# Two-layer attention decode: whole key blocks, one softmax for both head groups, queries made block-diagonal in PSUM, and an instruction order given as a table

## The chip, the cores and the metric

The kernel runs on 1 core of one Trainium2 chip. The metric is the device time of one run in microseconds (us), and of several runs the median.

## The reference

Two rounds of the same two layers with the same weights: attention of one new token per batch over a sliding window of cached keys and values, then a feed-forward layer, each with a layer norm ahead and a residual around it. All data are bfloat16.

```python
# B=8, Sq=1, D=448, Hq=16, Hkv=8, Sk=4096, Dh=256, F=1792
W = min(4096, max(256, Sk // 4))                      # 1024
q = (x @ wq).reshape(B, Sq, Hq, Dh)                   # two query heads per key head
k = jnp.repeat(k_cache[:, :, Sk - W:, :], 2, axis=1)  # v alike
p = softmax(einsum("bhqd,bhkd->bhqk", q, k) * Dh ** -0.5)
attn = einsum("bhqk,bhkd->bhqd", p, v).reshape(B, Sq, Hq * Dh) @ wo
ffn = silu(x @ w1) @ w2
x = x + attn(layernorm(x)); x = x + ffn(layernorm(x))
x = x + attn(layernorm(x)); x = x + ffn(layernorm(x))
```

The products, norms and residuals are small. The weights are some 10 MB, and the keys and values in the window 67 MB (8 batches of 8 heads of 1024 x 256, for keys and for values).

## The kernel before, in words

**Data.** Each batch's keys and values are 16 slots of 512 KB (one key head each). Both rounds use them, so they are loaded once, into a ring of 30 slots in SBUF ([128 x 2048] bfloat16 each). SyncE issues every DMA in one order: x, wq, the keys and values of batch 0, wo, w1, w2, and then K0..K7, V0..V7 of batches 1 to 7. A load waits until the slot that it takes is free: `layer2` (L1266) marks key slots as free after round 2's scores and value slots after round 2's products with values, and `pump` (L1229) then issues the next loads. Not more than 10 half slots are outstanding (`dma`, L656). `load_k` (L708) and `load_v` (L716) bring a slot as two halves of 256 KB with 2 KB rows. `load_wq` (L671) brings three full chunks of 1 MB and two pieces of 64 partitions, each 256 KB.

**One batch.** The batches are worked one after the other, with neighbours overlapped. Round 1 (`layer1`, L1240): VectorE turns each half key slot in place in 32 x 32 blocks of 32-bit words (L1246, 16 turns a batch). `scores` (L881) multiplies block-diagonal queries (`qbd`) with them: in round 1 both groups of four key heads in one product of 512 columns, in round 2 (layer 2 in the code) one group at a time, 256 columns. The softmax (L895 to L937) takes the row maximum on VectorE (L892), spreads it with two 32 x 32 turns (L900, L905), computes one exponential per head group on ScalarE (L912), turns the weights by products with the identity (`pT`, L918), copies them (`pTev`, L927) and sums them by eight small products (L931); a reciprocal follows (L936). The products with values are L951. Their result goes through a ScalarE copy (L956), another turn by products (L958) and VectorE copies (L965, L971) into `oT`; seven value heads take that way, the eighth goes by columns (L985, L991). Products with wo (L1002 by rows, L1008 by columns) add up in banks 6 and 7, `fold` (L1018, L1019) brings the rows into columns beside the residual (`x_init`, L997).

**Feed-forward and queries.** `xb_evac` copies the residual column in two steps (L1029 for 384 rows, L1030 for the last 64, which have a mask) and a third (L1057) for the second half of w1. `stat` (L1036, L1040) makes sums for the norm; `rsqrt` (L749 to L765) does the inverse root, on VectorE for the feed-forward's norm and on GpSimd for round 2's. w1 is L842, its turn L851, then L1063 to L1074 (tanh form of silu), and w2 is L1002 again. `chain` then copies the residual for the query product (L1086 to L1088), multiplies with wq in two head groups (L1104), turns the result (L1109), selects each head's part with four fp32 products (L1115), adds the mean's part on VectorE (L1121) and masks it into block-diagonal queries (L1129; VectorE for the first group, GpSimd for the second). Both groups of L1104 write bank 6, so the second waits for the first's turn. The exponential carries the norm's inverse deviation as its scale, and L909 scales the maximum.

**End.** Round 2's attention leaves `oT2` for all eight batches. `final` multiplies it with wo (L1135), starts the residual with a product (L1153), folds (L1165), copies (L1168 to L1172) and does the last feed-forward for all eight batches at once; the output leaves from L1219 and L1220.

**Order.** Each engine runs its own list in order; semaphores hold an instruction until what it needs is there. The lists come from a planner at build time (`Plan.schedule`, `tails`, `best_schedule`) that simulates the kernel with costs, shifted by hand-set numbers (`OFFSETS`, `MOVES`, `HOLDS`). Where the planner sees TensorE idle it places a filler (L1290): a product whose result nobody reads.

```python
        if last:
            softmax(b, 1, (k2,), sc, k2 == 1)
```

These two lines of `layer2` mean that the last batch runs round 2's softmax one head group at a time; all others run it once for both.

## Time and profile before

| | before |
|---|---|
| median of 3 runs | 241.93 us (241.26 to 241.96) |
| span of the profiled execution | 239.7 us |
| TensorE products (PE) | 194.1 us, 81%, 3567 of them, 129 fillers among them |
| TensorE weight loads (PEld) | 97.3 us, 41% |
| VectorE (DVE) | 152.8 us, 64%, 425 instructions |
| ScalarE (ACT) | 86.5 us, 36%, 292 |
| GpSimd (POOL) | 26.0 us, 11%, 125 |
| moved by DMA | 78.22 MB, mean 326 GB/s |
| mean granted TensorE clock | 0.986 of full speed |

The span goes from the first to the last instruction of one profiled execution; the run's time holds a little more. Busy time is what the instructions of an engine take; TensorE overlaps its products, and its weight loads run beside them. In the rows below, a line number names the kernel's line, `out<-in` its tiles, `x15` a count; after the bar stand the total busy time and the mean of one in ns, and after a second bar the time that the engine was idle ahead of them, with what released it. In tables by stretches, a row is a window in us, then its length and for PE, PEld, DVE, ACT and POOL the busy time (and instructions), the granted clock, the share of the 16 DMA engines and GB/s.

### The profile page before, as it was taken

How to read it: one execution, taken by the hardware profiler on the slowest of the kernel's cores; microseconds unless marked ns; L12 is line 12 of the kernel's file. 1: busy time of each engine (PE TensorE's matmuls, PEld its weight loads, DVE VectorE, ACT ScalarE, POOL GpSimd, SP SyncE). 2: the span in 40 equal slices, each digit the busy share in tenths (PEclk: the TensorE clock that was granted, in tenths of full speed). 3: DMA queues.
4: the chain of work that ended last, by engine and by line, in shares of the span. 5: the costliest groups of instructions: out<-in, count | busy, mean ns of one | idle time of the engine just before them, and what ended most of it. 6: DMA issues, size and time to landing. Idle time of an engine off the chain costs nothing.

```text
span 239.7 us, 8472 instructions
## 1 busy us (share of the span) xinstructions
PE 194.1 (81%) x3567; PEld 97.3 (41%) x3567; DVE 152.8 (64%) x425; ACT 86.5 (36%) x292; POOL 26.0 (11%) x125
## 2 busy tenths in 40 slices
PE   1052358878989899989898898989898999899894
PEld 1051123232345344535433453454344535445552
DVE  7339620037955995996599669946985996334533
ACT  2001231033045516532734354355416440544331
POOL 6100000002010031004001200310031003003000
PEclk9999985999999999999999999999999999999999
DMA  6999999999999999999999999999999999200000
GB/s 228 373 355 403 404 402 384 378 374 406 402 405 403 403 402 404 398 350 379 360 400 402 371 373 379 376 368 377 358 399 399 397 330 399 102 3 3 4 3 1
DMA packets 40341, 78.22 MB, mean 326 GB/s; under 512 B 4320, under 2 KB 6512, under 8 KB 39792
## 3 DMA queue, kind: packets, MB, share of 16 engines
q1 hardware_dynamic: 40304, 77.69, 87.2%
q8 instruction: 28, 0.46, 0.7%
q14 instruction: 9, 0.07, 0.1%
HBM read 77.67 MB, written 0.01 MB: 324 GB/s over the span
## 4 chain that ended last, share of the span: by engine, by line
PE 47%; DMA 19%; DVE 16%; ACT 7%; SPq 7%; issue 4%; POOL 0%; DVEq 0%; ACTq 0%
DMA ring<-in_A_k_cache_dram 10%; PE bank L951 9%; PE bank L881 7%; DMA w2o<-in_B_w_dram 6%; DVE ring L1246 6%; PE bank L1002 6%; PE bank L1290 5%; PE bank L1104 5%; PE bank L1115 3%; DMA ring<-in_A_v_cache_dram 3%; SPq L682 3%; ACT qT L912 2%; DVE mrow L892 2%; PE bank L918 2%; PE bank L958 1%
## 5 line engine op out<-in xcount | busy, mean ns | idle before, releaser
L1246 DVE STREAM_TRANSPOSE ring<-ring 128x512 uint32<-128x512 uint32 x128 | 81.4, 684 | 10.7 <-DMA ring<-in_A_k_cache_dram 10.7
L1290 PE MATMUL bank<-wq_sb,smalls 128*128 128x512 bf16 x129 | 38.6, 386 | 0.0
L881 PE MATMUL bank<-ring,qbd 128*16 128x512 bf16 (+2 forms) x768 | 35.8, 324 | 3.4 <-DVE ring L1246 2.3
L951 PE MATMUL bank<-ring,pT_sb 128*4 128x512 bf16 (+1 forms) x512 | 36.2, 378 | 0.1
L881 PEld LDWEIGHTS bank<-ring,qbd 128*16 128x16 bf16 (+1 forms) x768 | 19.6, 91 | 17.1 <-DVE qbd L1129 3.9
L858 ACT ACTIVATE qbd<-q1s 32x128 bf16<-32x128 bf16 x32 | 10.2, 320 | 42.9 <-PE bank L881 42.3
L892 DVE TENSOR_REDUCE mrow<-bank 128x2 f32<-128x512 f32 (+1 forms) x17 | 11.0, 646 | 11.9 <-PE bank L881 11.1
L1104 PE MATMUL bank<-wq_sb,xn 128*4 128x512 bf16 (+1 forms) x272 | 17.7, 369 | 0.9 <-ACT x2s L1091 0.5
L1018 ACT ACTIVATE qT<-bank 128x448 bf16<-128x448 f32 x16 | 8.7, 543 | 22.4 <-PE bank L1002 22.4
L951 PEld LDWEIGHTS bank<-ring,pT_sb 128*4 128x4 bf16 (+1 forms) x512 | 11.5, 84 | 11.1 <-issue 1.8
L1290 PEld LDWEIGHTS bank<-wq_sb,smalls 128*128 128x128 bf16 x129 | 10.2, 98 | 12.3 <-issue 7.6
L918 PE MATMUL bank<-ident,qT 128*64 128x16 bf16 x256 | 8.5, 180 | 7.3 <-ACT qT L912 6.6
L1002 PE MATMUL bank<-w2o,oT 128*1 128x448 bf16 x224 | 13.2, 352 | 0.7 <-DMA w2o<-in_A_wo_dram 0.7
L956 ACT ACTIVATE qT<-bank 128x512 bf16<-128x512 f32 x16 | 9.6, 597 | 9.7 <-PE bank L951 6.7
L1109 DVE STREAM_TRANSPOSE qT<-bank 128x512 f32<-128x512 f32 (+1 forms) x17 | 11.3, 664 | 2.2 <-PE bank L1104 2.0
L918 PEld LDWEIGHTS bank<-ident,qT 128*64 128x64 bf16 x256 | 6.1, 111 | 12.5 <-ACT qT L912 11.5
L956 ACT ACTIVATE qbd<-bank 128x512 bf16<-128x512 f32 (+1 forms) x16 | 9.1, 570 | 5.5 <-PE bank L951 3.3
L749 POOL TENSOR_SCALAR smalls<-smalls 128x1 int32<-128x1 int32 x8 | 1.5, 190 | 86.9 <-ACT smalls L1051 76.3
L1257 POOL MEMSET qT<- 128x64 bf16 x8 | 1.2, 152 | 82.5 <-PE bank L958 68.7
L1115 PE MATMUL bank<-qT,w2o 128*32 128x64 f32 x128 | 8.4, 352 | 2.0 <-DVE qT L1109 0.8
L912 ACT ACTIVATE qT<-bank,mrow 128x256 bf16<-128x256 f32 x17 | 7.2, 470 | 7.6 <-DVE mrow L905 7.3
L1046 DVE SCALAR_TENSOR_TENSOR smalls<-bank,smalls 128x1 f32<-128x1 f32 x8 | 1.1, 143 | 13.2 <-ACT smalls L1044 9.5
(183 smaller groups left out, 254.6 us busy)
## 6 DMA issues: line engine op xcount, KB each, us to landing
ring<-in_A_k_cache_dram SPq DMA_DIRECT2D x128, 256.0 KB, 6.2
ring<-in_A_v_cache_dram SPq DMA_DIRECT2D x128, 256.0 KB, 6.1
w2o<-in_A_wo_dram SPq DMA_DIRECT2D x2, 1792.0 KB, 13.1
wq_sb<-in_A_wq_dram SPq DMA_DIRECT2D x3, 1024.0 KB, 6.8
w2o<-in_B_w_dram SPq DMA_DIRECT2D x1, 1568.0 KB, 14.5
w_sb<-in_B_w_dram SPq DMA_DIRECT2D x3, 448.0 KB, 12.2
wq_sb<-in_A_wq_dram SPq DMA_DIRECT2D x2, 256.0 KB, 10.2
w_sb<-in_B_w_dram SPq DMA_DIRECT2D x2, 112.0 KB, 11.4
```

The lines of the kernel that those rows point to most:

```text
L881: fns.append(lambda e, cb=cb, par=par, j=j, kv=kv, m=m, c0=c0, c1=c1: e.matmul(bank[sc][32 * j:32 * j + m, c0:c1], qbd[layer][:, j * 8 + c ...
L892: dve(lambda e: e.tensor_reduce(mseg[layer][:, ks[0]:ks[-1] + 1], bank[sc][:, lo:hi].rearrange("p (k n) -> p k n", k=len(ks)), AX.X, ALU.m ...
L912: act(lambda e, k2=k2: e.activation(e_sb[ei][:, k2, :, :].rearrange("p uh (jj ul) -> p uh jj ul", ul=2), bank[sc][:, k2 * 256:(k2 + 1) * 2 ...
L918: pe([lambda e, uh=uh, ql=ql, k2=k2: e.matmul(bank[lb][64 * ql:64 * ql + 64, k2 * 64:k2 * 64 + 64].rearrange("p (j q u r) -> p u j q r", j ...
L951: fns.append(lambda e, qh=qh, uh=uh, j=j, vv=vv: e.matmul(bank[ob][32 * j:32 * j + 2 * w, 0:w * DH], p_col(ei, k2, j, qh, uh, w), vv, star ...
L956: act(lambda e: e.activation(o_sb[oi][:, 0:w * DH], bank[ob][:, 0:w * DH], ACTF.Copy), bk(ob), O_K[oi], 0.2 + w * 0.2, "oevh" if ob == OB[ ...
L1002: pe([lambda e, i=i, c=c: e.matmul(bank[XB][32 * c:32 * c + 1, 0:D], rhs(i), w_sb[:, i * D:(i + 1) * D], start=(first and i - i0 < 4), sto ...
L1104: fns.append(lambda e, j=j, c=c, wb=wb, off=off, h0=h0, n=n, k2=k2: e.matmul(bank[wb][32 * j:32 * j + 4, h0:h0 + n], xn[:, part(c, k2), j, :],
L1109: dve(lambda e, wb=wb, h0=h0, n=n: e.transpose(qT[:, h0:h0 + n].rearrange("p (c a i) -> p c a i", a=2, i=32), bank[wb][:, h0:h0 + n].rearr ...
L1115: pe([lambda e, qs=qs, j=j: e.matmul(qs[32 * j:32 * j + 32].rearrange("p (k c r) -> p k r c", k=4, c=8), irep, qT[:].rearrange("p (r c i) ...
L1246: dve(lambda e, v=v: e.transpose(v, v), [("slot", s, h)], [("slot", s, h)], 0.67, "KT")
L1290: fills = {n: [lambda e, j=j, m=P // n: e.matmul(bank[OB[0]][m * j:m * j + m, 0:2 * DH], zero_b.broadcast_to([P, m]), wq_sb[:, 0:2 * DH], ...
```

## The change

- **Keys whole.** `load_k` brings a slot in one DMA of 512 KB with 4 KB rows. VectorE turns a slot in one instruction of 128 x 1024 words, 8 a batch. `load_v` stays. The second 64-partition piece of wq is issued from ScalarE's queue at the program's start.
- **One softmax area.** Both head groups' scores add into the same 256 columns of a bank (other rows are zero through padded queries), in round 1 too, where 64 products of 256 columns replace 32 of 512. One maximum, one exponential (which also sums its row), one set of eight turning products; one fp32 product with a selection matrix makes the sums that eight made.
- **Block-diagonal in PSUM.** The second head group of wq writes bank 4, the first bank 6. Eight fp32 products, four with the mean's part (which ScalarE writes into `qbd`) and four with the turned query, make the block-diagonal queries in bank 5; one ScalarE copy with the inverse deviation as its scale moves them to `qbd`. The addition and masking on VectorE and GpSimd go, and so do L909 and the exponential's scale.
- **Residual in five columns.** The last 64 rows have a column for each half of the partitions, so that one copy replaces two or three (`xb_evac`, the copy for wq, the copy in `final`); `x_init`, products by columns and folds work on five columns. In `final` the residual is added behind the wo products.
- **Norms.** GpSimd's inverse root takes five steps instead of nine.
- **Order.** The planner goes. `ORDER` gives each engine's list as task numbers, and `place` reads it; `f` words are fillers, 101 instead of 129.

```diff
-    AHEAD, WHOLE = 10, 0
+    AHEAD = 10
 def load_k(s, b, kvh):
-        for h in range(2):
-            dma(lambda e, h=h: e.dma_start(slots[s][:, 1024 * h:1024 * h + 1024], src[:, 1024 * h:1024 * h + 1024]),
-                [("slot", s, h)], W * DH, "slot%d_%d" % (s, h), rate=400e3, ahead=AHEAD)
+        dma(lambda e: e.dma_start(slots[s], src), [("slot", s, h) for h in range(2)], 2 * W * DH, "slot%d" % s,
+            rate=418e3, ahead=AHEAD)
 def load_wq():
-                [("wq", 3 + h)], D3 * HD, "wq%d" % (3 + h), rate=220e3)
+                [("wq", 3 + h)], D3 * HD, "wq%d" % (3 + h), via=("sp", "act")[h])
 def layer1(b):
-            for h in range(2):
-                v = slots[s][:, h * 1024:(h + 1) * 1024].bitcast(U32)
-                dve(lambda e, v=v: e.transpose(v, v), [("slot", s, h)], [("slot", s, h)], 0.67, "KT")
-        for ks in ((0, 1),) if PAIR0 else ((0,), (1,)):
-            scores(b, 0, ks, SC[0])
+            v = slots[s].bitcast(U32)
+            dve(lambda e, v=v: e.transpose(v, v), [("slot", s, 0), ("slot", s, 1)], [("slot", s, 0), ("slot", s, 1)],
+                1.22, "KT")
+        for k2 in range(2):
+            scores(b, 0, k2, SC[0])
 def softmax(b, layer, ks, sc):
+        act(lambda e: e.activation(
+            e_sb[ei].rearrange("p uh (jj ul) -> p uh jj ul", ul=2),
+            bank[sc][:, 0:256].rearrange("p (ul uh jj) -> p uh jj ul", ul=2, uh=4), ACTF.Exp, bias=mseg[layer][:, 0:1],
+            scale=1.0, accum_out=es), bk(sc) + [("mseg", layer)], [("e", ei), ek], 0.55, "exp%d" % layer)
+        pe([lambda e: e.matmul(bank[lb][:, C_L + 8 * k0:C_L + 8 * k1], es.broadcast_to([P, P]), sel16[:, 8 * k0:8 * k1],
+                               start=True, stop=True)], [ek] + SEL16, bk(lb), (256, 1), "l%d" % layer)
 def xb_evac():
-        act(lambda e: e.activation(xbt[:, 0:3, 0], xcols()[:, 0:3], ACTF.Copy), bk(YB), [("xbt", 0)], 0.175, "xbt")
-        act(lambda e: e.activation(xbt[:, 3, 0:1], xcols()[:, 3:4], ACTF.Copy, scale=mask4[:, 3:4]), bk(YB) + MASK4,
-            [("xbt", 1)], 0.175, "xbt")
+        act(lambda e: e.activation(xbt[:, :, 0], xcols(), ACTF.Copy), bk(YB), ["xbt"], 0.175, "xbt")
 def chain(b):
-            parts = [(XB, 0, DH), (YB, DH, DH)] if (tail or WQS) and k2 == 0 else [(XB, 0, 2 * DH)]
+            wbs = [(XB, 0, DH), (LB[0], DH, DH)] if tail and k2 == 0 else [((XB, XB if tail else LB[0])[k2], 0, 2 * DH)]
...
+            for part_ in range(2):
+                for j in range(4):
+                    rhs = qT[:].rearrange("p (r c i) -> p i c r", r=2, i=32)[:, 0:4] if part_ else \
+                        csm[:, k2].rearrange("p (j c) r -> p j c r", j=4)
+                    fns.append(lambda e, j=j, rhs=rhs, part_=part_: e.matmul(
+                        qs[32 * j:32 * j + 32].rearrange("p (k c q r) -> p q k c r", k=4, c=8, q=4)[:, j], irep, rhs,
+                        start=not part_, stop=bool(part_), tile_position=(0, 32 * j)))
+            act(lambda e, k2=k2: e.activation(qbd[1][:, k2], qs.rearrange("p (n x) -> p n x", x=8), ACTF.Copy,
+                                              scale=rstds[1]), bk(LB[1]) + [("rstd", 1)], [("qbd", 1, k2)], 0.4, "qbd")
 ORDER = ...
+        "47 54 66 73 146 76 147+6 81 159+1 173+1 164+3 169 175+1 f1@168 f1@168 f1@106@168 163 f1@168 f2@168 178 "
...
-    pl.best_schedule(fill)
+    pl.place(fill)
```

In the fences below a row is an instruction's line, operation, tiles, shape and count. The first place is on VectorE, in batch 4's feed-forward norm; `ring` are key slots of batch 5 that are turned, `smalls` hold the norm's numbers, and bank 7 holds the sums. Before:

```order
L1246 STREAM_TRANSPOSE ring<-ring 128x512 x5
L1046 SCALAR_TENSOR_TENSOR smalls<-bank7,smalls 128x1
L749 TENSOR_SCALAR smalls<-smalls 128x1
L754 SCALAR_TENSOR_TENSOR smalls<-smalls 128x1
L1246 STREAM_TRANSPOSE ring<-ring 128x512
L760 SCALAR_TENSOR_TENSOR smalls<-smalls 128x1
L851 STREAM_TRANSPOSE qT<-bank6 128x2x224
L754 SCALAR_TENSOR_TENSOR smalls<-smalls 128x1
L1063 SCALAR_TENSOR_TENSOR vt<-cs1,smalls,qT 128x14
L760 SCALAR_TENSOR_TENSOR smalls<-smalls 128x1
```

Now:

```order
L990 STREAM_TRANSPOSE ring<-ring 128x1024 x3
L802 SCALAR_TENSOR_TENSOR smalls<-bank7,smalls 128x1
L513 TENSOR_SCALAR smalls<-smalls 128x1
L518 SCALAR_TENSOR_TENSOR smalls<-smalls 128x1
L531 SCALAR_TENSOR_TENSOR smalls<-smalls 128x1
L620 STREAM_TRANSPOSE qT<-bank6 128x2x224
L518 SCALAR_TENSOR_TENSOR smalls<-smalls 128x1
L818 SCALAR_TENSOR_TENSOR ffn<-ffn,smalls,qT 128x14
L531 SCALAR_TENSOR_TENSOR smalls<-smalls 128x1
```

Half-slot turns that stood partly among the norm's steps (five ahead, one between) are now three whole turns, all ahead of it.

The second place is on TensorE, around batch 4's product of the feed-forward with w2 (`hT` or `ffn` on the right, bank 6). `qbd1` is also the buffer for the turn of attention's output (L958, now L705), and `pT_sb1` are round 2's weights of batch 3. Before:

```order
L951 MATMUL bank1<-ring,pT_sb1 4x512 x8
L931 MATMUL bank5<-pT_sb1,smalls 128x16 x8
L1290 MATMUL bank2<-wq_sb,smalls 128x512
L958 MATMUL bank5<-ident,qbd1 128x8 x4
L1002 MATMUL bank6<-w2o,hT 1x448 x14
L958 MATMUL bank5<-ident,qbd1 128x8 x4
L1290 MATMUL bank2<-wq_sb,smalls 128x512 x2
```

Now (the w2 product is the row of L753, and L645 are round 1's scores of batch 5, which write bank 0):

```order
L698 MATMUL bank1<-ring,pT_sb1 4x512 x4
L645 MATMUL bank0<-ring,qbds 16x256 x8
L705 MATMUL bank5<-ident,qbds 128x8 x4
L645 MATMUL bank0<-ring,qbds 16x256 x8
L705 MATMUL bank5<-ident,qbds 128x8 x4
L753 MATMUL bank6<-w2o,ffn 1x448 x14
L645 MATMUL bank0<-ring,qbds 16x256 x16
```

The scores of batch 5 with its first four key heads' slots now begin ahead of the w2 product; before they began after it (next fence).

The third place follows right behind on TensorE: batch 4's queries for round 2 (L1104 with wq, now L857; L1115 the selection, now L872), up to the scores. Before:

```order
L1104 MATMUL bank6<-wq_sb,xn 4x512 x16
L1036 MATMUL bank5<-xbt 128x32 x4
L1040 MATMUL bank5<-smalls 128x16
L997 MATMUL bank7<-xb0,ident 128x64
L1290 MATMUL bank2<-wq_sb,smalls 128x512
L1115 MATMUL bank5<-qT,w2o 32x4x2x8 x4
L1104 MATMUL bank6<-wq_sb,xn 4x512 x16
L881 MATMUL bank1<-ring,qbd1 8x256 x32
L881 MATMUL bank0<-ring,qbd0 16x512 x8
L1115 MATMUL bank5<-qT,w2o 32x4x2x8 x4
L881 MATMUL bank0<-ring,qbd0 16x512 x24
```

Now:

```order
L792 MATMUL bank5<-ffn 128x32 x4
L796 MATMUL bank5<-smalls 128x16
L857 MATMUL bank6<-wq_sb,xn 4x512 x16
L857 MATMUL bank4<-wq_sb,xn 4x512 x8
L645 MATMUL bank0<-ring,qbds 8x256 x24
L872 MATMUL bank5<-qbds,w2o 32x32x2 x4
L872 MATMUL bank5<-qT,w2o 32x32x2 x4
L645 MATMUL bank0<-ring,qbds 8x256 x8
L857 MATMUL bank4<-wq_sb,xn 4x512 x8
L645 MATMUL bank1<-ring,qbds 16x256 x32
L872 MATMUL bank5<-qbds,w2o 32x32x2 x4
L872 MATMUL bank5<-qT,w2o 32x32x2 x4
```

The second group of wq products stands right behind the first, in another bank, with scores of batch 5 (L645 into bank 0) ahead of the selection; each selection has four products with `qbds` (the mean's part) and four with `qT`.

More of the change, by code (lines that the diff above doesn't have):

```diff
@@ L1 @@
-import heapq
 import numpy as np
@@ L1017, in fold @@
     def fold():
[L1018 to L1021 removed]
+        act(lambda e: e.activation(rowb, bank[XB][:, 0:D], ACTF.Copy), bk(XB), ["rowA"], 0.545, "rowb")
```

616 lines of the change are left out of this document (184 added, 432 removed), and 89 rows, old and new, of tables (MOVES, OFFSETS, ORDER).

## The prediction

> **What bounds the kernel now.** I read the page, the chain that ended last, the busy time of the engines by stretches, the waits, and the timelines of one batch and of the end. The page gives the span.
>
> ```profile
> span 239.7 us, 8472 instructions
> ```
>
> The median of the three runs shown is 241.93 us, so 2.2 us lie around the profiled span. I make the sum against the span and add 2.2. The runs lie between 241.26 and 241.96, so about 0.3%, 0.7 us, can be told from no change.
>
> The chain that ended last, in order of time (start, length, what), shows the milestones.
>
> ```profile
> 54.00 0.94 PE bank L1002 x14
> 68.98 0.70 DVE mrow L892
> 202.32 0.70 DVE mrow L892
> 205.45 1.25 PE bank L951 x19
> 237.47 0.38 DVE ring L1219
> ```
>
> L1002 at 54.00 is the first product with w2: until then the kernel waits for weights. L892 is the row maximum of layer 1, for batch 1 at 68.98 and for batch 7 at 202.32. L951 at 205.45 is batch 7's first product with its values, and L1219 is the last copy. So there are three stretches: a head of 68.98 us, six equal periods, and a tail of 37.4 us. The busy times over the six periods (length, then PE, PEld, DVE, ACT, POOL, granted clock, DMA share, GB/s), first, last and sum:
>
> ```profile
> 68.98:91.63 22.65, 20.52 (x390) 10.07 (x379) 17.14 (x45) 10.10 (x35) 2.70 (x11) 1.00 1.05 403
> ...
> 180.90:202.32 21.42, 19.90 (x395) 10.26 (x383) 17.32 (x48) 10.18 (x34) 2.61 (x11) 1.00 1.02 380
> sum 133.34, PE 121.79 PEld 60.64 DVE 103.08 ACT 60.55 POOL 15.72; mean PE 20.30 PEld 10.11 DVE 17.18 ACT 10.09 POOL 2.62
> ```
>
> A period is 133.34 / 6 = 22.22 us. TensorE is busy for 20.3 us of it, but the fillers (products that nobody reads) are in that:
>
> ```profile
> L1290 PE MATMUL bank<-wq_sb,smalls x61: 375/378/392, 69.8 to 197.1; 128*128 128x512 bf16 x61
> ```
>
> Sixty-one of them, ten a period, mark where TensorE has nothing to do and waits for a softmax, a residual copy or a turned query. The transfers are not the first bound: in the last period they run at 380 GB/s, and the waits between 69 and 202 us say why (the first is SyncE's queue, from 90 us on; us in total, times, longest).
>
> ```profile
> SPq L713 <- PE bank L951: 11.5, 5, 3.1
> DVE ring L1246 <- DMA ring<-in_A_k_cache_dram: 2.7, 4, 1.1
> ```
>
> Key loads wait 11.5 us for slots that layer 2 still reads; VectorE's turns wait only 2.7 us for keys. So a period is the serial path of one batch through TensorE, VectorE and ScalarE, and the stream follows it. What the change takes off that path counts six times.
>
> **The head.** Rates by stretches (last column GB/s):
>
> ```profile
> 6.00:8.00 2.00, 0.48 (x12) 0.40 (x12) 1.25 (x9) 0.00 (x0) 1.06 (x10) 1.00 1.02 426
> 10.00:12.00 2.00, 0.00 (x0) 0.00 (x0) 0.00 (x0) 0.00 (x0) 0.00 (x0) 1.00 1.01 266
> 12.00:14.00 2.00, 0.13 (x5) 0.16 (x6) 0.00 (x0) 0.00 (x0) 0.00 (x0) 1.00 1.02 255
> 56.00:58.00 2.00, 1.65 (x23) 0.69 (x24) 1.34 (x3) 1.42 (x11) 0.31 (x2) 1.00 1.05 406
> ```
>
> At 6 to 8 us whole rows of wq (8 KB each) move at 426 GB/s; at 56 to 58 half slots (2 KB rows) at 406. Between them, at 10 to 14, stand the two 64-partition pieces of wq, at some 260. The change issues one of these (256 KB) from ScalarE's queue at the start, beside full-width rows: at 426 it takes 0.62 us instead of 1.01, a gain of 0.4. Bounds: 0, if the piece slows its neighbours as much, and 0.75, if the piece left behind also runs at 426. The Trainium skill, DMA: Bandwidth & Descriptors (section Issuing engines are not separate DMA queues), says that DMAs from several engines interleave on the same 16 engines and that a second issuer saves only sequencer time; by that rule this term is 0 and the sum below 0.4 us higher. No run so far has two issuers, so the trace cannot decide it.
>
> Whole key slots have 4 KB rows. One of 16 engines takes 2048 B x 16 / 406 = 81 ns for a 2 KB row and 308 ns for 8 KB; a straight line between gives 156 ns for 4 KB, 419 GB/s. Keys of one batch (4.19 MB) then take 10.0 us instead of 10.3: 0.32 us for batch 0 and again for batch 1 (bounds: 0 at 406, 0.5 at 426). The turns:
>
> ```profile
> L1246 DVE STREAM_TRANSPOSE ring<-ring 128x512 uint32<-128x512 uint32 x128 | 81.4, 684 | 10.7 <-DMA ring<-in_A_k_cache_dram 10.7
> ...
> 60.79 5.44 DVE L1246 STREAM_TRANSPOSE ring<-ring 128x512 uint32<-128x512 uint32 x9
> ```
>
> Nine in a row take 5.44 us, so 605 ns apart though each lasts 684. The launch that a whole turn saves is at least nothing and, by this overlap, some 0.08 us: eight pairs, 0.6 us a batch. Against it, the last slot lands whole and its turn lasts about 1.2 us instead of 0.68: 0.5 later. Layer 1's scores add 0.2 (below). These three cancel to +0.1. Head: -0.4 - 0.32 - 0.32 + 0.1 = -0.9.
>
> **A period.** Costs in layer 1's softmax:
>
> ```profile
> L892 DVE TENSOR_REDUCE mrow<-bank 128x2 f32<-128x512 f32 x15 | 10.1, 675 | 11.1 <-PE bank L881 10.3 <-POOL qbd L1129 0.8
> L892 DVE TENSOR_REDUCE mrow<-bank 128x1 f32<-128x256 f32 x2 | 0.8, 425 | 0.8 <-PE bank L881 0.8
> L912 ACT ACTIVATE qT<-bank,mrow,smalls 128x256 bf16<-128x256 f32 x15 | 7.8, 560 | 0.3
> ...
> 114.94 0.84 ACT L912 ACTIVATE qT<-bank,mrow 128x256 bf16<-128x256 f32 x2
> ```
>
> Both head groups now lie in 256 columns: the maximum falls from 675 to 425 ns (-0.25), and two exponentials (0.84 together) become one. It also sums its row, which no row here shows; I take the dearer 256-column form, 0.56 (-0.28). TensorE's rows of batches 2 and 3, from its timeline:
>
> ```profile
> 116.50 0.37 PE L931 MATMUL bank<-pT_sb,smalls 128*128 128x16 bf16 x8
> 116.80 1.89 PE L951 MATMUL bank<-ring,pT_sb 128*4 128x512 bf16 x28
> ...
> 129.66 0.38 PE L1290 MATMUL bank<-wq_sb,smalls 128*128 128x512 bf16 x1
> 130.70 0.53 PE L1115 MATMUL bank<-qT,w2o 128*32 128x64 f32 x8 [0.66 <-ACT x2s L1091]
> ...
> 132.16 1.06 PE L881 MATMUL bank<-ring,qbd 128*8 128x256 bf16 x32
> 133.15 0.39 PE L1290 MATMUL bank<-wq_sb,smalls 128*128 128x512 bf16 x1
> 133.47 0.61 PE L881 MATMUL bank<-ring,qbd 128*16 128x512 bf16 x8
> 133.91 0.52 PE L1115 MATMUL bank<-qT,w2o 128*32 128x64 f32 x8
> 134.21 2.52 PE L881 MATMUL bank<-ring,qbd 128*16 128x512 bf16 x56
> ```
>
> Starts, not ends, are to be read, since products overlap. The eight sums (L931) hold TensorE for 0.30 us; one fp32 product takes their place, by an eighth to a quarter of L1115's time about 0.1: -0.2 in each layer, -0.4. The query selection (L1115, four fp32 products in eight records) holds it for 0.30 to 0.53 us; it now has eight products, the second four adding the mean's part in PSUM, and all eight stand behind the turned query. I take +0.4 each, twice: +0.8. Layer 1's scores were 32 products of 512 columns at 55 ns (0.44 / 8), 1.76 us; they become 64 of 256 at 31 ns (0.99 / 32), 1.98: +0.22. The fifth residual column adds six small products, at 31 ns +0.19. TensorE's own work grows by 0.81.
>
> Its gaps shrink. From 129.66 to 130.70 it had a filler and a wait of 0.66, since the second weight group shared bank 6 with the first and had to wait until that was turned. The change gives it bank 4, and next batch's scores stand there too (last pair of order fences): -1.04. The residual is copied once:
>
> ```profile
> L1030 ACT ACTIVATE xbt<-bank,smalls 128x1 bf16<-128x1 f32 x16 | 4.1, 258 | 0.1
> ```
>
> On the path to layer 2's statistics and weights -0.26. With softmax, -0.25 - 0.28 - 0.26 - 1.04 = -1.83. VectorE also loses the query's addition and masking, and GpSimd its masking; ScalarE's one copy of 256 columns replaces them while TensorE works on the second group, so I price that at 0 (about 0.5 a period if that cover goes). A period: 22.22 + 0.81 - 1.83 = 21.2; six of them, -6.1.
>
> Next bound: w2 lands just ahead of 54.00, now near 53.2. Seven batches of keys (29.4 MB at 419) and values (at 406) take 70.1 + 72.3 us, so the stream cannot end before 195.6; by the forecast batch 7's values are wanted from 197.7 to 200. It fits, barely.
>
> **The tail.**
>
> ```profile
> 217.31 0.36 PE L1013 MATMUL bank<-w2o,smalls 128*128 128x448 bf16 x1
> 218.36 0.39 PE L1290 MATMUL bank<-wq_sb,smalls 128*128 128x512 bf16 x1
> 220.08 0.41 PE L1153 MATMUL bank<-x2s,ring 128*128 128x28 f32 x2
> 222.23 0.41 DVE L1129 TENSOR_TENSOR qbd<-mrow,smalls 128x256 bf16<-128x256 f32 x1
> 223.25 0.30 ACT L909 ACTIVATE mrow<-mrow,smalls 128x2 f32<-128x2 f32 x1 [2.01 <-DVE mrow L905]
> 230.91 0.26 ACT L1169 ACTIVATE ring<-bank,smalls 128x8 bf16<-128x8 f32 x1
> ```
>
> These steps stand on the last chain and go: a filler product (0.36), another (0.32 of it), the residual's start (0.35, moved behind the last wo products), a masking that stood ahead of the maximum's transposes (0.41), the scaled bias (0.30, since queries now carry the scale), and a masked copy (0.26). With the layer 1 softmax (0.73, the sum included), layer 2's two sums (0.4) and one residual copy (0.26): -3.39. Against that +0.37 for twelve small products and +0.4 for one selection. Tail: -2.6. The scaled query needs the inverse deviation earlier; GpSimd's nine steps for it become five, which I price at 0 (0.3 if late).
>
> **Sum.** -0.9 - 6.1 - 2.6 = -9.6; span 230.1, time 232.3.
>
> **The rivals.**
> *The stream takes over.* If gaps close further (VectorE is relieved of 0.6 us in turns besides), a period falls to the stream's 20.4 and the end is set by 195.6: batch 7's values 4 us earlier than forecast, 228. For it: 403 GB/s in the first period; against it, the slot waits. Chance 0.16.
> *The gaps move instead of closing.* TensorE's added 0.81 and new waits eat what is saved: a period stays at 22.2, only head and tail gain: 238.4. For it: TensorE is already busy 20.3 of 22.2. Chance 0.20, 0.03 of it with no change at all.
> *Late keys hold the path (slower).* Layer 1's scores of batch 5 now stand ahead of batch 4's w2 product, and three whole turns ahead of its statistics (order fences). Both engines take instructions in order, so a late key slot holds batch 4's path, which frees the slots later still. Price: the longest turn wait was 1.1 us; two such a period make 2.2, six periods 13.2: 245.5. It decides from 9.6 / 6 = 1.6 us a period on. Against it: 2.7 us of such waits in all six now. Chance 0.12.
> *The clock drops.*
>
> ```profile
> 24.00:26.00 2.00, 0.17 (x7) 0.20 (x8) 2.00 (x4) 1.59 (x5) 0.00 (x0) 1.00 1.05 406
> 36.00:38.00 2.00, 1.29 (x18) 0.33 (x13) 0.17 (x1) 0.60 (x1) 0.00 (x0) 0.50 1.05 389
> ```
>
> TensorE, busy 0.17 of 2 us at 24, ran at half clock at 36. The change has 101 fillers instead of 129; if one stretch of some 7 us in the tail ran at half clock, 3.5 us: 235.8. The Trainium skill, TensorE: Matmul & The Clock Gate (section HAM oscillation), says that idle gaps longer than about 3.4 us halve the clock; the six periods have none and show 1.00. Chance 0.06.
>
> **How the numbers follow.** The forecast has 0.44 (230 to 235); 0.02 is left for the rest. Faster: 0.44 + 0.16 + 0.17 + 0.06 + 0.01 = 0.84; within 0.3%: 0.04; slower: 0.12. The range goes from the stream's bound, 227.5, to the case of moved gaps with its next microsecond, 239.5, and leaves the slower case out. Should the change not do what it says, keys at 4 KB moving no faster than 406, the head loses 0.64 and the stream's bound 2.3: 232.9, inside it.
>
> **What would show it.** Maxima of layer 1 about 21.2 us apart, batch 7's near 195; selections that hold TensorE 0.7 to 0.9 us; key loads near 419 GB/s; a tail near 34.8. Wrong: a period at 22 or more, VectorE's turns waiting for keys by many microseconds, a tail no shorter, or a granted clock below 1.00 after 70 us.

## The result and the profile after

The changed kernel takes 257.37 us, median of 4 runs (255.59 to 261.7), against 241.62 us (4 runs, 241.26 to 241.96) of the kernel before: a ratio of 1.0627, 95% interval 1.058 to 1.0674. The forecast was 232.3 us, so time was lost where 9.6 us were to be gained. Executions more than 1.5% above the fastest of their kernel are left out of the ratios but not of the medians in us (five of E16's twelve, three of E10's ten, and three of E9's four, which therefore has no ratio).

The page of the kernel after:

```profile
span 255.3 us, 8580 instructions
PE 203.5 (80%) x3758; PEld 109.4 (43%) x3758; DVE 138.9 (54%) x340; ACT 78.3 (31%) x251; POOL 15.8 (6%) x67
PEclk9999999997999799999999999999999999997999
...
L990 DVE STREAM_TRANSPOSE ring<-ring 128x1024 uint32<-128x1024 uint32 x64 | 76.1, 1218 | 14.2 <-DMA ring<-in_A_k_cache_dram 14.1
```

The work did shrink where it was meant to: VectorE from 152.8 to 138.9 us, ScalarE from 86.5 to 78.3, GpSimd from 26.0 to 15.8. TensorE grew from 194.1 to 203.5 although it has 26 fillers fewer (103; two of the table's 101 words stand for two products). The clock row, by slices of 6.4 us, has three slices at 7 tenths, one each in the head, the periods and the tail, and the key turns waited 14.1 us for keys.

VectorE's timeline of after shows the milestones (start, length, what; in brackets the idle time ahead and what ended it). L655 is the row maximum, here of batch 0, batch 1 and batch 7, before at 31.50, 68.98 and 202.32:

```profile
17.52 1.25 DVE L990 STREAM_TRANSPOSE ring<-ring 128x1024 uint32<-128x1024 uint32 x1 [12.73 <-DMA ring<-in_A_k_cache_dram]
...
19.38 0.16 DVE L566 COPY xb<-bank 64x8 bf16<-64x8 bf16 x1
...
40.12 0.42 DVE L655 TENSOR_REDUCE mrow<-bank 128x1 f32<-128x256 f32 x1 [6.78 <-PE bank L645]
...
75.96 0.42 DVE L655 TENSOR_REDUCE mrow<-bank 128x1 f32<-128x256 f32 x1
...
215.37 0.43 DVE L655 TENSOR_REDUCE mrow<-bank 128x1 f32<-128x256 f32 x1 [0.76 <-PE bank L645]
```

So the head is 7.0 us longer (75.96 against 68.98), the six periods 6.1 (139.41 against 133.34, 23.24 us each against 22.22), the tail 2.5 (39.9 against 37.4): 15.6 us of span. The first two rows show the head's reason. VectorE stands 12.73 us for a key slot before it makes the last copy of x (L566), which the kernel before made at 4.53:

```profile
4.53 0.16 DVE L800 COPY xb<-bank 64x8 bf16<-64x8 bf16 x1
```

TensorE in the head of after:

```profile
21.16 0.27 PE L542 MATMUL bank<-xb,smalls 128*128 128x8 bf16 x4 [17.25 <-DVE ring L539]
...
21.50 3.55 PE L505 MATMUL bank<-xb,wq_sb 128*128 128x9 bf16 x128
```

The first norm (L542) and the first query product (L505) wait for that copy; before, the same product began when wq's third chunk had landed:

```profile
13.87 3.56 PE L741 MATMUL bank<-xb,wq_sb 128*128 128x9 bf16 x128 [7.07 <-DMA wq_sb<-in_A_wq_dram]
```

The periods by stretches, of after (first, last, sum; columns as before):

```profile
75.96:100.94 24.98, 23.38 (x418) 12.42 (x417) 15.38 (x35) 8.96 (x29) 1.42 (x5) 0.93 0.93 346
...
194.06:215.37 21.31, 19.32 (x365) 10.31 (x366) 15.67 (x35) 8.65 (x28) 1.41 (x5) 1.00 1.00 374
sum 139.41, PE 126.79 PEld 67.97 DVE 91.99 ACT 53.87 POOL 8.50; mean PE 21.13 PEld 11.33 DVE 15.33 ACT 8.98 POOL 1.42
```

VectorE lost 1.85 us a period and ScalarE 1.11, yet the periods are longer. TensorE is the engine that gained (20.30 to 21.13 us, with fewer fillers). Its timeline shows where: the fold (L778) and the products by columns with wo in a period, and those with w2 in the tail, of after,

```profile
158.13 0.36 PE L778 MATMUL bank<-smalls,qT 128*128 128x16 bf16 x5 [0.22 <-ACT qT L774]
158.43 1.25 PE L763 MATMUL bank<-oT,w2o 128*128 128x16 bf16 x20
...
229.89 1.84 PE L763 MATMUL bank<-ffn,w2o 128*128 128x16 bf16 x30
```

and of before (the fold is L1019):

```profile
77.50 0.26 PE L1019 MATMUL bank<-smalls,qT 128*128 128x16 bf16 x4
77.62 0.55 PE L1008 MATMUL bank<-oT,w2o 128*128 128x16 bf16 x16
...
215.48 0.74 PE L1008 MATMUL bank<-hT,w2o 128*128 128x16 bf16 x24
```

A quarter more products take more than twice the time, and they stand ahead of every batch's statistics. Last, the second stretch at half clock, in windows of 1 us of after (the clock is the third number from the end):

```profile
83.00:84.00 1.00, 0.75 (x16) 0.19 (x12) 0.89 (x2) 0.20 (x1) 0.00 (x0) 1.00 1.04 426
84.00:85.00 1.00, 0.60 (x11) 0.51 (x11) 1.00 (x2) 0.34 (x1) 0.00 (x0) 1.00 1.05 422
85.00:86.00 1.00, 1.00 (x21) 0.82 (x19) 0.55 (x1) 0.01 (x1) 0.00 (x0) 1.00 0.98 385
86.00:87.00 1.00, 1.00 (x16) 0.32 (x16) 0.00 (x0) 0.17 (x1) 0.00 (x0) 0.52 0.60 246
...
88.00:89.00 1.00, 1.00 (x11) 0.24 (x7) 0.93 (x4) 0.48 (x3) 0.00 (x0) 0.50 0.90 365
```

From 86 to about 89.5 TensorE runs at 0.50. That costs half of it, some 1.7 us, if TensorE is what is waited for; the kernel has three such stretches.

### The profile page after: what moved, and what is told of

It is laid out like the page before. It is cut to its first block, busy times and chain, and to the rows that moved or that the text cites. A ratio compares the mean times of both kernels' runs of the same rounds, so it can differ in the third digit from the quotient of the medians.

```text
span 255.3 us, 8580 instructions
## 1 busy us (share of the span) xinstructions
PE 203.5 (80%) x3758; PEld 109.4 (43%) x3758; DVE 138.9 (54%) x340; ACT 78.3 (31%) x251; POOL 15.8 (6%) x67
## 4 chain that ended last, share of the span: by engine, by line
PE 64%; DVE 11%; ACT 10%; DMA 6%; issue 5%; POOL 3%; SPq 0%; ACTq 0%
PE bank L645 12%; PE bank L698 11%; PE bank L1034 8%; PE bank L753 7%; PE bank L763 4%; DMA ring<-in_A_k_cache_dram 4%; DVE ring L990 3%; PE bank L857 3%; PE bank L611 3%; DMA wq_sb<-in_A_wq_dram 2%; PE bank L872 2%; ACT qbds L876 2%; PE bank L677 2%; PE bank L778 2%; PE bank L705 2%
## 5 line engine op out<-in xcount | busy, mean ns | idle before, releaser
L990 DVE STREAM_TRANSPOSE ring<-ring 128x1024 uint32<-128x1024 uint32 x64 | 76.1, 1218 | 14.2 <-DMA ring<-in_A_k_cache_dram 14.1
L645 PE MATMUL bank<-ring,qbds 128*16 128x256 bf16 (+1 forms) x1024 | 39.1, 286 | 6.4 <-ACT qbds L876 4.4
L698 PE MATMUL bank<-ring,pT_sb 128*4 128x512 bf16 (+1 forms) x512 | 38.6, 381 | 1.6 <-issue 1.0
L1034 PE MATMUL bank<-wq_sb,smalls 128*128 128x512 bf16 (+1 forms) x103 | 33.6, 419 | 0.0
L645 PEld LDWEIGHTS bank<-ring,qbds 128*16 128x16 bf16 (+1 forms) x1024 | 25.0, 90 | 18.4 <-ACT qbds L876 10.0
L655 DVE TENSOR_REDUCE mrow<-bank 128x1 f32<-128x256 f32 x17 | 7.2, 425 | 23.8 <-PE bank L645 23.8
L857 PE MATMUL bank<-wq_sb,xn 128*4 128x512 bf16 (+1 forms) x272 | 19.8, 395 | 0.4 <-ACT xn L840 0.3
L698 PEld LDWEIGHTS bank<-ring,pT_sb 128*4 128x4 bf16 (+1 forms) x512 | 11.9, 84 | 13.0 <-issue 2.4
L876 ACT ACTIVATE qbds<-bank,smalls 128x256 bf16<-128x256 f32 x16 | 7.6, 474 | 26.8 <-PE bank L872 19.2
L1034 PEld LDWEIGHTS bank<-wq_sb,smalls 128*128 128x128 bf16 (+1 forms) x103 | 8.7, 105 | 15.2 <-issue 12.5
L703 ACT ACTIVATE qT<-bank 128x512 bf16<-128x512 f32 x16 | 9.6, 598 | 15.8 <-PE bank L698 14.3
L542 PE MATMUL bank<-xb,smalls 128*128 128x8 bf16 x4 | 0.3, 174 | 17.3 <-DVE ring L539 17.3
L753 PE MATMUL bank<-w2o,oT 128*1 128x448 bf16 x224 | 13.3, 352 | 0.0
L627 ACT ACTIVATE qbds<-q1s 32x128 bf16<-32x128 bf16 x32 | 10.1, 316 | 2.9 <-PE bank L645 2.2
L703 ACT ACTIVATE qbds<-bank 128x512 bf16<-128x512 f32 (+1 forms) x16 | 9.1, 567 | 4.6 <-PE bank L698 3.9
L763 PE MATMUL bank<-oT,w2o 128*128 128x16 bf16 (+1 forms) x160 | 10.0, 183 | 0.0
L611 PE MATMUL bank<-w_sb,ffn 128*1 128x448 bf16 (+1 forms) x128 | 9.7, 383 | 0.3 <-ACT ffn L787 0.3
```

The source lines that it names most:

```text
L611: pe([lambda e, i=i, k=k, c=c: e.matmul(bank[bi][32 * c:32 * c + n, 0:FN], lhs(k), w1_sb[:, i * F + c * FN:i * F + (c + 1) * FN] if i < 3 else
L627: act(lambda e, q=q: e.activation(qbd[0][32 * q:32 * q + 32].rearrange("p k n (q r) -> p k n q r", r=2)[:, :, :, q, :], q1s[32 * t:32 * t ...
L645: fns.append(lambda e, cb=cb, par=par, j=j, kv=kv[:, cb, par], m=8 if k2 else 16: e.matmul(bank[sc][32 * j:32 * j + m, 0:256], q_l(layer, ...
L698: fns.append(lambda e, qh=qh, uh=uh, j=j, vv=vv: e.matmul(bank[ob][32 * j:32 * j + 2 * w, 0:w * DH], p_col(ei, k2, j, qh, uh, w), vv, star ...
L703: act(lambda e: e.activation(o_sb[oi][:, 0:w * DH], bank[ob][:, 0:w * DH], ACTF.Copy), bk(ob), O_K[oi], 0.2 + w * 0.2, "oevh" if ob == OB[ ...
L753: pe([lambda e, i=i, c=c: e.matmul(bank[XB][32 * c:32 * c + 1, 0:D], rhs(i), w_sb[:, i * D:(i + 1) * D], start=(first and i - i0 < 4), sto ...
```

## The experiments

Theory 1: the order at the head costs the head, and the new TensorE forms cost the periods. Theory 2: it is the scaled copy of the queries, which now waits for GpSimd's inverse root. Theory 3: it is the order table as a whole.

**E1, the first norm ahead of the key turns.** In VectorE's list at the start, the copy for the first norm (50) and the norm's steps go ahead of batch 0's key turns (138 to 145):

```diff
-        "3 11 14 4 13 49 5 48 8 140 9 50 138 52+1 7 6 55+2 18 143 58 17 144 20 141 59 16 67 142 60 71 61 68 72 62 "
-        "145 63 12 69 19 15 64+1 139 70 154+1
+        "3 11 14 4 13 49 5 48 8 9 50 52+1 7 6 55+2 58+7 18 17 20 16 12 19 15 138 139 140 67 68 69+1 71+1 141 142 "
+        "143 144 145 154+1
```

> The changed kernel with one difference: in VectorE's list the steps of the first norm (all 8 batches at once) stand ahead of batch 0's key turns again, as they did before the change. Theory 1 (in the changed kernel the turn of the third key slot stands ahead of them and waits 12.7 us for its DMA, so the first queries, and with them everything, come late): the first row maximum moves from 40.1 to about 32 us, the one of batch 1 from 76.0 to about 69, and the time falls by 7 us, from 257.4 to about 250. Rival (the head is late because whole key slots land later and the products with wq are late anyway): the first maximum stays above 38 us and the time moves by less than 2 us.

252.76 us, 1.0425 (1.0377 to 1.0473): 4.6 us of the 15.7 (4.9 by the ratios) are the order of one list at the start. E1's query product on TensorE, and its first maximum on VectorE:

```profile
14.68 3.55 PE L505 MATMUL bank<-xb,wq_sb 128*128 128x9 bf16 x128 [7.93 <-DMA wq_sb<-in_A_wq_dram]
```

```profile
29.26 0.42 DVE L655 TENSOR_REDUCE mrow<-bank 128x1 f32<-128x256 f32 x1 [1.98 <-PE bank L645]
```

The first maximum comes 10.9 us earlier than in after and 2.2 earlier than before, but batch 1's comes at 69.09, as before (68.98): in E1's chain that ended last, the head now waits 14.65 us for wo, until 44.25. So 7 us of the head were mended, yet only 4.6 came through: in this profile the six periods grew by 2.9 us, to 142.3. In the same chain, batch 6 waits for values:

```profile
184.22 7.11 DMA ring<-in_A_v_cache_dram
```

**E2 and E3, the copy freed from GpSimd.** The query copy loses its scale; the exponential gets it, and a ScalarE copy scales the maximum (as L909 did before). E2 is that alone, E3 together with E1's list.

```diff
-            act(lambda e, k2=k2: e.activation(qbd[1][:, k2], ..., ACTF.Copy, scale=rstds[1]), bk(LB[1]) + [("rstd", 1)], ...
+            act(lambda e, k2=k2: e.activation(qbd[1][:, k2], ..., ACTF.Copy), bk(LB[1]), ...
```

> The changed kernel with one part undone: the copy that makes block-diagonal queries has no scale, and the exponential carries the norm's inverse deviation again (with the scaled maximum ahead of it, 0.3 us on ScalarE). Theory 2 (the copy waits for GpSimd's five steps, 7.6 us in five batches, and round 2's scores wait for the copy): these waits vanish, and 4 to 7 us go: 250 to 253. Rival (the copy would be late anyway, for the selection's products): the wait only changes its name, and the time moves by less than 1.5 us.

> Both edits at once (norm first, scale in the exponential). If both theories hold and the losses add, 257.4 - 7 - 5 = 245 us, still above the kernel before at 241.6, and what is left lies in the periods' order and in stretches of TensorE at half clock. If the structure of the change (eight-product selections, whole key turns) is what costs, it stays above 252.

256.92 us, 1.0636 (1.0589 to 1.0682), and 253.17 us, 1.0499 (1.0462 to 1.0535): nothing gained, alone or together. The waits of that copy (us in total, times, longest) in after, and then in E3, where it is L889:

```profile
ACT qbds L876 <- PE bank L872: 19.2, 9, 3.1
...
ACT qbds L876 <- POOL smalls L528: 7.6, 5, 2.0
```

```profile
ACT qbds L889 <- PE bank L885: 25.3, 14, 3.1
```

The 7.6 us for GpSimd are gone, and the wait for the selection grew from 19.2 to 25.3. A wait is put down to what came last; the selection came nearly as late. Theory 2 falls.

**E4, E5 and E13, whose order?** E4 gives the changed work to the old planner, without its hand-set moves; E5 is the kernel before without these moves; E13 is E4 with E6's grouping (below).

```diff
-    pl.place(fill)
+    pl.best_schedule(fill)
```

> The changed kernel's own tasks in an order made by the planner of the kernel before (its costs, its offsets by name and its fillers, without the list of single moves), in place of the table. Theory 3 (the table's order is at fault, not the tasks): the first maximum comes near 32 us, the periods come below 22.5 us, and the time falls to 240 to 247 us though nobody tuned this order. Rival (the tasks themselves are the loss): 250 us or more, with periods of 23 us.

> The kernel before, with its planner's list of single moves left out: its tasks in the same kind of order as e13_planner_cols has. It tells what the two sets of tasks cost under one planner that was tuned for neither by hand. If the changed tasks are the better ones once the columns are grouped, it comes above e13_planner_cols (252 or more); if they are worse, below it (243 to 247).

> As e4_planner (the changed tasks in the old planner's order, 256.5 us), with the products by columns grouped by shape as in e6_cols. If the shape changes cost the same whatever the order, 5 to 7 us less: 249 to 251. If it was the table's order that made them dear, less than 3 us.

E4 takes 256.45 us (1.0619, 1.0578 to 1.0661), E5 248.77 (1.0308, 1.0243 to 1.0372), E13 251.37 (1.0409, 1.0334 to 1.0485). With an order that has no late head (first maximum at 29.74 us) the changed work is as slow as with the table. Under one planner without moves the new work is 7.7 us slower than the old, of which E13 gives back 5.1. Where the difference lies, the six periods and the tail tell, of E4 and then of E5:

```profile
69.72:209.83 140.11, 121.49 (x2440) 66.73 (x2458) 93.89 (x206) 53.29 (x171) 8.41 (x30) 1.00 0.98 365
209.83:253.10 43.27, 33.89 (x632) 19.69 (x637) 12.42 (x53) 12.38 (x42) 1.78 (x6) 1.00 0.08 28
```

```profile
69.25:208.22 138.97, 118.31 (x2306) 59.01 (x2330) 104.26 (x273) 59.90 (x204) 15.45 (x66) 1.00 1.00 365
208.22:246.50 38.28, 30.24 (x663) 17.42 (x666) 15.56 (x60) 14.13 (x49) 2.58 (x13) 1.00 0.09 33
```

The periods differ by 1.1 us and the tail by 5.0: in E4 the last batch's second maximum comes 4.9 us behind its first (231.33 and 236.25), in E5 1.6 and with the table 2.2. So most of this gap lies in the tail, whose order was made with numbers set for the old work; how much of it the new work itself costs, these runs don't tell. In the periods the table's order is no worse than the planner's: grouped, they take 137.9 us in E13 and 137.6 with the table (E6). There theory 3 falls.

**E6, products by columns grouped by shape (on E1).** Of the five columns three are whole products (128 output partitions), two half ones (64). The change did them in turn for each input; E6 does all whole ones, then all half ones.

```diff
-        for i in ins:
-            for c in range(XC):
+        for cs_ in ((0, 1, 2), (3, 4)):
+            for i, c in [(i, c) for i in ins for c in cs_]:
```

> As e1_norm_first (252.8 us), and the products by columns are put in another order: for all inputs first the 128-row pieces, then the 64-row pieces, in place of three and two by turns. Theory A (a change between 128-row and 64-row products costs TensorE time: 20 such products took 1.25 us, the 16 of the kernel before 0.55, and 30 of them 1.84 where 24 took 0.74): 20 products fall to 0.75 us, a period by 0.4 to 0.5, and the whole by 3 to 5 us, to 248 to 250. Rival (64-row products are slow by themselves, or there is slack): the 20 still take 1.1 us or more, or the time moves by less than 1 us.

245.39 us, 1.0148 (1.0085 to 1.0211): 7.4 us less than E1 (6.7 by the ratios), with the same products. TensorE's rows of E6, in a period and in the tail:

```profile
149.93 0.69 PE L763 MATMUL bank<-oT,w2o 128*128 128x16 bf16 x20
...
220.81 0.90 PE L763 MATMUL bank<-ffn,w2o 128*128 128x16 bf16 x30
```

Four inputs in turn change shape 7 times, grouped once: 1.25 - 0.69 us over 6 changes. Six inputs change 11 times, grouped once: 1.84 - 0.90 over 10. That is 0.093 and 0.094 us a change, the same price from both. The Trainium skill, TensorEngine Tiling (Array Packing), section Key Properties, says that changing the tiling mode drains TensorE; these rows fit that and give a change a price, though they don't show that a drain is what takes the time. Eight batches of 0.56 and 0.94 in the tail make 5.4 us, which is what E4 to E13 gained (5.1). E1 to E6 gained more; E1's profile has three half-clock stretches, and E6's page has one left, which may be the rest but was not separated:

```profile
PEclk9999999999999999979999999999999999999999
```

**E7 and E8, more fillers against the half clock.** Two more fillers ahead of each fold, on E1 (E7) and on E6 (E8).

```diff
+                for t in [t for t in out if t.name == "fold"]:
+                    for _ in range(2):
+                        out.insert(out.index(t), f)
```

> As e1_norm_first, and two fillers more ahead of every fold (where TensorE waits some 0.6 us for ScalarE's copy of the rows), 32 in all. Theory B (the table's 101 fillers leave stretches in which TensorE streams too little, and each costs 3.4 us at half clock, 1.7 us of TensorE's time, two or three times in a run): no granted clock below 1.00 after 60 us, and 2 to 5 us less, 248 to 251. Rival (the half clock falls into waits, or the fillers delay the folds): dips go and the time stays, or dips stay.

> Both of e6_cols and e7_fill. If both theories hold the gains add, 5 to 9 us below e1_norm_first: 244 to 248. If TensorE's work is not what sets the period, it stays above 250.

254.94 us (1.0518, 1.0443 to 1.0592) and 247.53 (1.0226, 1.0164 to 1.0287): by the medians each some 2 us above the kernel that it was made from, though the intervals touch. E7's page still has such stretches:

```profile
PEclk9999996599999999999999999999997999997999
```

E8's profile shows 1.00 throughout, and it is no faster for it. At best these fillers gained nothing.

**E9, keys in halves again (on E1).** `load_k` in two DMAs and two turns, as before the change.

```diff
...
-            dve(lambda e: e.transpose(v, v), ..., 1.22, "KT")
+            for h in range(2):
+                dve(lambda e, v=v: e.transpose(v, v), [("slot", s, h)], [("slot", s, h)], 0.67, "KT")
```

> As e1_norm_first, with the keys in halves again (two DMAs and two turns a slot, one behind the other in VectorE's list). If whole key slots help as the prediction has it (0.3 to 0.6 us for the keys of batches 0 and 1, 0.6 us a batch of VectorE's time that nobody waits for): 0.5 to 1.5 us slower, 253 to 254.5. Rival (whole slots land late and hold VectorE): 1 us or more faster.

Four runs, 249.59 to 255.1 us, median 254.96: nothing follows, so no run tells what whole key slots alone are worth.

**E10 and E14, the mean's part of the selection (on E6).** E10 leaves the four products with the mean's part out; E14 keeps them, in bfloat16 instead of float32.

```diff
-            for part_ in range(2):
+            for part_ in (1,):
```

```diff
-    csm = qz[1][:, 8:].bitcast(F32).rearrange("p (k n x) -> p k n x", k=2, x=4)[:, :, :, 0:2]
+    csm = qz[1][:, 8:].rearrange("p (k n x) -> p k n x", k=2, x=8)[:, :, :, 0:2]
...
-                        ...[:, j], irep, rhs,
+                        ...[:, j], irep if part_ else ident[:, 0:32], rhs,
```

> As e6_cols (245.4 us), but the selection has only its four products with the turned query; the four with the mean's part are left out, so round 2's queries lack the mean's term. The prediction priced the four at 0.4 us a selection, 0.8 a period, 6.4 in all: by it 239. Rival (products of one shape one behind the other overlap; the starts in the changed trace leave 0.1 us each): 1 to 2 us, 243.5 to 245.

> As e6_cols (245.4 us), with the four products of the mean's part in bfloat16 (identity in place of the fp32 selector), so that all work is kept. If it is the fp32 passes of these four that cost the 2 to 3 us which e10_sel4 gave back: 242.5 to 244. If it is the number of products and their wait for ScalarE's copy of the mean's part: 245 or more.

243.07 us (10 runs), 1.0019 (0.9975 to 1.0062), and 244.1 us (12 runs), 1.0095 (1.006 to 1.013). Left out it gains 2.3 us on E6 (3.1 by the ratios), cheaper it gains 1.3; by their intervals E14 is not told from E6. TensorE's rows of the selection in E6 and in E14:

```profile
134.35 0.31 PE L872 MATMUL bank<-qbds,w2o 128*32 128x64 f32 x8
134.47 0.50 PE L872 MATMUL bank<-qT,w2o 128*32 128x64 f32 x8
```

```profile
110.74 0.23 PE L872 MATMUL bank<-qbds,ident 128*32 128x64 bf16 x4
110.78 0.52 PE L872 MATMUL bank<-qT,w2o 128*32 128x64 f32 x8
```

By the starts, the mean's part holds TensorE for 0.12 us in float32 (eight records for four products) and 0.04 in bfloat16, not for its length.

**E11, bank 6 for both query groups again (on E6).** This undoes the second bank, and puts the second group's products behind the first selection.

```diff
-            wbs = [...] if tail and k2 == 0 else [((XB, XB if tail else LB[0])[k2], 0, 2 * DH)]
+            wbs = [...] if tail and k2 == 0 else [(XB, 0, 2 * DH)]
```

> As e6_cols, but the second weight group of round 2's queries writes bank 6 again, behind the first group's selection, as before the change. The prediction priced the other bank at 1.04 us a period: by it 6 to 7 us slower, 252. Rival (TensorE serves two batches there, and what it no longer waits for it spends on scores that come next anyway): less than 2 us slower, 245 to 247.

244.94 us, 1.0112 (1.0044 to 1.018), against E6's 1.0148: no loss where 6 to 7 us were forecast. The second bank gains nothing that these runs can tell (their intervals leave room for some 1.4 us). The six periods of E6 and of E11 by stretches:

```profile
69.24:206.82 137.58, 120.30 (x2396) 65.54 (x2412) 92.09 (x203) 53.84 (x173) 8.49 (x30) 0.99 0.98 366
```

```profile
69.57:205.58 136.01, 119.85 (x2394) 66.62 (x2411) 92.35 (x203) 53.84 (x173) 8.41 (x30) 1.00 1.00 370
```

22.9 and 22.7 us a period; E6 holds one half-clock stretch, some 1.7 us in six periods, which is all of that difference.

**E15, the late head in the kernel before.** In the hand-set moves of VectorE's list, its last copy of x (L800) goes behind one key turn, and nothing else.

```diff
-        "1652:1650 ...
+        "164:57 1652:1650 ...
```

> The kernel before with one entry more in its list of moves: the turn of the third key slot's second half stands ahead of the copy that feeds the first norm, as a key turn does in the changed kernel. If that order alone makes the head late: the first maximum moves from 31.5 to 37 to 40 us, and the time grows by 4 to 7 us, to 245 to 248. Rival (the kernel before waits for w2 until 54 us anyway, so its head has room): under 2 us.

246.53 us, 1.0198 (1.0149 to 1.0246), from one instruction. VectorE's timeline of E15:

```profile
17.30 0.71 DVE L1246 STREAM_TRANSPOSE ring<-ring 128x512 uint32<-128x512 uint32 x1 [12.93 <-DMA ring<-in_A_k_cache_dram]
...
18.15 0.16 DVE L800 COPY xb<-bank 64x8 bf16<-64x8 bf16 x1
...
37.07 0.69 DVE L892 TENSOR_REDUCE mrow<-bank 128x2 f32<-128x512 f32 x1 [3.43 <-PE bank L881]
```

The same wait (12.93 us) and the same late first maximum (31.50 before) in a kernel that has nothing else of the change.

**E16, half products first (on E14).** A fold ends on half products; the products by columns behind it now begin with theirs.

```diff
-        for cs_ in ((0, 1, 2), (3, 4)):
+        for cs_ in ((3, 4), (0, 1, 2)):
```

> The version with the bf16 mean part, with one edit: the products by columns take their half products (64 output partitions) first and their whole ones (128) behind. Theory A (a change between whole and half products costs TensorE a fixed time): the runs so far give it as 1.25 - 0.69 us over six changes fewer and 1.84 - 0.90 over ten fewer, 0.093 and 0.094 us a change. The fold ahead of them ends on half products, so two changes a batch go, 0.19 us: from the fold's start to the end of the products by columns 0.98 us (0.29 + 0.69 before) become about 0.79, and if that path counts in all eight batches the median falls by up to 1.5 us, from 1.0095 of the kernel before to about 1.003 to 1.007. Theory B (the 0.56 and 0.94 us came from something else in the alternating order, such as the weights' places in memory, and a change of shape as such is free): the same 0.98 us, 1.0095 again. Either way what stays above the kernel before bears on where the last 2.3 us lie, since the five-column fold itself holds a change that the four-column one did not (fold to products 0.29 us against 0.11).

243.34 us (12 runs), 1.0033 (0.9997 to 1.0069). TensorE's rows of E14 and of E16, fold and products by columns of batch 1 (granted clock 1.00 in both):

```profile
78.22 0.36 PE L778 MATMUL bank<-smalls,qT 128*128 128x16 bf16 x5 [0.65 <-ACT qT L774]
78.51 0.69 PE L763 MATMUL bank<-oT,w2o 128*128 128x16 bf16 x20
```

```profile
77.25 0.36 PE L778 MATMUL bank<-smalls,qT 128*128 128x16 bf16 x5 [0.65 <-ACT qT L774]
77.47 0.67 PE L763 MATMUL bank<-oT,w2o 128*64 128x16 bf16 x20
```

From the fold's start to the last product's end 0.98 us became 0.89, and to the start of what follows (L698, at 79.12 and 78.06) 0.90 became 0.81: one change of 0.09 went, not the two that the expectation counted. The order of shapes alone moved it, so the expectation's theory B falls. By the ratios E16 is 0.6 points below E14, but eight times 0.09 us are only 0.3, the intervals overlap (1.006 and 1.0069), and by the medians (243.34 against 241.58, 244.1 against 241.8) it is 0.2 points.

The ladder of ratios: after 1.0627, E1 1.0425, E6 1.0148, E14 1.0095, E16 1.0033. The mended kernel stands level with the kernel before, or up to 0.7% above it; none that does all the work is faster.

## Why the prediction was wrong

The loss came mainly from two terms, the head's (1) and the fifth column's (2), each shown by undoing it. Why the forecast gain did not come either is item 6, and stays open in part.

1. "Head: -0.4 - 0.32 - 0.32 + 0.1 = -0.9" measured +7.0. The terms were rates and launches; the order of VectorE's list at the start, which the change moved too, was not read, though the order fences showed turns put ahead of norm steps for batch 4. E1 and E15 show it from both sides: one wait for keys ahead of one copy, 4.6 us of median here, 2% in the old kernel too. With it undone the head was as before (69.09), so the 0.9 us of gains did not come either. The rival "late keys hold the path" named the mechanism and priced it in the periods; it sat in the head, where 12.73 of the 14.1 us of VectorE's key waits are. In the periods those waits stayed small.
2. "The fifth residual column adds six small products, at 31 ns +0.19": the price of a product was right, the price of alternating was left out. Measured +0.70 a batch (1.25 against 0.55) and, in the tail, 1.84 against 0.74. The folds changed too: from the fold's start to the products behind it 0.12 us before and 0.30 after, by its two changes of shape. At 7 changes in the products by columns, one back, and four around two folds, some 12 a batch make about 1.1 us (an estimate from 0.093). By E6's 7.4 us this is the largest failed term.
3. "The clock drops", priced at 3.5 us for the tail and given 0.06: it did drop, three times, some 1.7 us each, once in the tail. The one shown above began at 86.0, right behind the alternating products (from 84.69 on), in which TensorE was busy 0.60 to 1.00 of each microsecond. The Trainium skill, TensorE: Matmul & The Clock Gate (section HAM oscillation), speaks of idle gaps over about 3.4 us; the rows show no such gap. That small products count as little work is argued from the places, not shown: E7's fillers did not remove the stretches, and E14, with its products grouped, still has one in the tail (0.50 at 221 to 224 us). What sets them off stays open.
4. "The change gives it bank 4 ...: -1.04" did not come: E11, without the bank, is no slower.
5. "I take +0.4 each, twice: +0.8" for the selections was right in sign, but two to three times too dear: E10's 2.3 us (3.1 by the ratios) over eight batches are 0.3 to 0.4 a batch.
6. "So a period is the serial path of one batch through TensorE, VectorE and ScalarE" is the premise that failed. VectorE and ScalarE were relieved by 3 us a period together, yet the shortest period of a run that does all the new work is E14's, 135.70 / 6 = 22.6 us, and E16, with TensorE's losses mostly mended, is only back at the time of before. What was taken off two engines did not come back as time. TensorE's own work rose; that the overlap of neighbouring batches hid the rest is argued, not shown. TensorE's groups in the six periods give the fillers' busy time, in before and in after (the first number after the bar):

```profile
L1290 PE MATMUL bank<-wq_sb,smalls 128*128 128x512 bf16 x61 | 19.6, 381 | 0.0
```

```profile
L1034 PE MATMUL bank<-wq_sb,smalls 128*128 128x512 bf16 x54 | 17.0, 391 | 0.0
```

   Two more fillers of after have another shape (0.4 us). Without them all a period held (121.79 - 19.6) / 6 = 17.0 us of TensorE's work before and (126.79 - 17.4) / 6 = 18.2 after, so some 1.2 us more where 0.81 was forecast; 0.3 of it is the half-clock stretch from 86 us on. What exactly sets 22.2 us was not isolated, and one rival is left: the kernel before has an order with moves set by hand, worth 3% to it (E5), and no run gave the new work such an order.
7. "Which I price at 0 (0.3 if late)" for GpSimd's root: the wait came (7.6 us in all), and removing it gained nothing (E2, E3).

The softmax and the residual copy, priced at -0.53 and -0.26 a period, were not tested by themselves. Right were the rates. Rates of after at the start (last column GB/s):

```profile
10.00:12.00 2.00, 0.00 (x0) 0.00 (x0) 0.00 (x0) 0.00 (x0) 0.00 (x0) 1.00 1.00 338
12.00:14.00 2.00, 0.00 (x0) 0.00 (x0) 0.00 (x0) 0.00 (x0) 0.00 (x0) 1.00 1.02 295
14.00:16.00 2.00, 0.00 (x0) 0.00 (x0) 0.00 (x0) 0.00 (x0) 0.00 (x0) 1.00 1.02 418
```

4 KB rows move at 418 GB/s (419 forecast), one maximum takes 0.42 us. The piece of wq on ScalarE's queue lifted the rate at 10 to 14 us to 338 and 295 from 266 and 255, but the query product came at 14.68 in E1 against 13.87, so the -0.4 was +0.8; 0, by the rule that the prediction cited from the Trainium skill (DMA: Bandwidth & Descriptors, section Issuing engines are not separate DMA queues), was nearer.

## What to carry to other kernels

When a change replaces a planner by a table, read the list of every engine from its first instruction: one wait that stands ahead of a small copy cost 2%. Count changes between product shapes as well as products, and keep equal shapes together. A wait removed from an engine is worth time only if nothing else comes nearly as late.

## What was not expected of the hardware

A change between products with 128 and with 64 output partitions took TensorE 0.093 us (20 products 1.25 and 0.69 us, 30 products 1.84 and 0.90). TensorE fell to a granted clock of 0.50 for about 3.4 us though its records show it busy 0.75, 0.60 and 1.00 in the three microseconds ahead. More fillers ahead of the folds bought nothing back (E7, E8).
